# One core, attention into an ELU network: the first batch's q in paired slots with 128x128 transposes, k's maxima spread by a copy in place of diagonals, and two exchanges in the order of loads and weights

## The chip, the cores and the metric

The kernel runs on one core of a Trainium2 chip. The metric is the device time of one execution in microseconds (us). The engines that matter here: TensorE (PE in the profile, with its weight loads as PEld), VectorE (DVE), ScalarE (ACT), GpSimd (POOL) and SyncE (SP). SP and POOL also issue the loads: SP those of q, k and v, POOL those of the two weight matrices.

## The reference

q, k and v are float32 of 8 batches, 8 heads, 576 tokens and 64 columns; w_in is 512 x 2048 and w_out 2048 x 512.

```python
q_s = np.exp(q - np.max(q, axis=-1, keepdims=True))
q_s = q_s / (np.sum(q_s, axis=-1, keepdims=True) + 1e-09)
k_s = np.exp(k - np.max(k, axis=2, keepdims=True))
k_s = k_s / (np.sum(k_s, axis=2, keepdims=True) + 1e-09)
kv = np.einsum('bhsd,bhse->bhde', k_s, v)
attn = np.einsum('bhsd,bhde->bhse', q_s, kv)
x = attn.transpose(0, 2, 1, 3).reshape(8 * 576, 512)
h = x @ w_in
g = np.where(h > 0.0, h, np.exp(np.minimum(h, 0.0)) - 1.0)
out = g @ w_out
```

q's softmax runs over the 64 columns of a head, k's over the 576 tokens: k's maximum is one number for each head and column.

## The kernel before

Every batch's attention is computed while the network of the batch before it runs. The network works in steps, 16 for each batch: in a step, four hidden products (`hidden`, L912) make 128 of the 2048 hidden columns for 512 tokens, ACT, POOL and DVE apply the ELU, and four output products (`project`, L933) of an earlier step follow, three steps behind. The remaining 64 tokens of every batch are gathered and run at the end as a ninth block. PE does these products from about 20 us to the end.

The order of everything else is written out by hand. `START` lists, word by word, what is issued ahead of the first step; each engine takes its own words in that order and waits on semaphores for what it reads. `FIRST`, `SECOND` and `LATER` list, for each of the 16 steps, what is put in after the hidden products, after the output products and after the ELU. Words such as `load:Q:0:1` (load slot 1 of batch 0's q, issued by SP), `w1:14:16` (load chunks 14 and 15 of w_in, issued by POOL), `qmax`, `qsub`, `qexp`, `qsum`, `qmul` (the steps of q's softmax) and `att`, `xc` (q times kv, and its copy to XT, the input of the network) stand for methods of that name.

**The first batch.** Its q, k and v lie in four slots each. A slot holds two heads, one on partitions 0 to 63 and one on 64 to 127; a partition holds 9 tokens of its head, 8 of which belong to the 512 and one to the rest. Slot x holds heads 2x and 2x+1. Half A is slots 0 and 1, half B slots 2 and 3.

**q.** DVE takes the maxima (L672), POOL or DVE subtracts them (L679), ACT takes the exponential (L684), DVE sums (L689), and POOL or DVE multiplies by the reciprocal into QS (L708). `qturn_slots` transposes QS on PE (L766) so that the 64 columns of two partner heads lie on the partitions: four 64x64 transposes for each of the 8 tokens of a half, and eight for the rest (`pturn0:R`, in step 10). ACT copies the result to QT (L788; the rest L855).

**k.** `kmax_first` takes the maximum over a slot's 9 tokens on DVE in four steps (L326): 8 tokens to 4, to 2, to 1, and the ninth. `kturn_first` transposes the result on PE (L331), and DVE takes the maximum over the 64 partitions of a head, negated, into NM (L337): one number for each column on the partitions, a column of NM for each head of the slot pair. To subtract it, the maximum must be spread over all tokens. `kdiag` on ACT writes NM on the diagonal of a 128x128 block, one for each of the two columns (L368). `kraw_first` had put k itself into PSUM by a product with the identity (L513), and `kmin_first` adds the negated maxima there: two products for each bank (L524), with the stationary matrices HALF0 and HALF1 (ones in one half of the columns, zeros in the other) and the diagonal blocks as the moving side. A bank holds 512 columns, or 128 for the ninth tokens (parts S and T). ACT takes the exponential out of PSUM (L538, L533).

`kspread` (L465) does the same for batch 1 in step 8: two products of 256 columns, which ACT copies to NB.

**kv and what follows.** `kv_first` (L560) makes kv of a half. It needs k's exponential of that half and v's copy in bf16: `vconv:A` on ACT (L855), `vconv:B` on POOL (L857). `kv_fac` takes the reciprocal of the sums on DVE (L614) and scales kv into MB, half A on DVE (L629), half B on ACT (L623). `att` (L805) multiplies with QT, and `xc` copies to XT (ACT L814, DVE L812).

**POOL's order in the start**: subtraction of q's slot 0, the loads of w_in chunks 1 to 3 and 0, of w_out 0 and 1, of w_in 4 and 5, the subtractions of slots 2 and 3, two more weight loads, `vconv:B`, the last two multiplications of q.

Of the kernel before, what the change touches and what calls it, by code (L numbers as in the profile page):

```python
# [15 lines left out]
R = 4  # L16
# [25 lines left out]
START = ("load:Q:0:1 load:K:0:0 load:K:0:1 warm:1:7 warm:4:7 qmax:1 warm:2:4 load:Q:0:3 qsub:1:dve "  # L42
# [13 lines left out]
    4: ("w1:12:14", "w2:9:11 w2:11:13", "load:K:1:R qsum:A qsub0:R:dve"),  # L56
    5: ("w1:14:16", "kturn", "kacross vconv:R qmax:C"),
# [63 lines left out]
class Gen:  # L121
# [57 lines left out]
    def alloc(self):  # L179
# [4 lines left out]
        self.HALF = [a(f"HALF{i}", [128, 128], F32R) for i in range(2)]  # L184
# [27 lines left out]
        self.DG = a("DG", [128, 4, 128], F32R)  # L212
        self.NM = a("NM", [128, 4], F32)
        self.QM = a("QM", [128, 36], F32)
# [13 lines left out]
    def init(self):  # L228
# [17 lines left out]
        for i in range(2):  # L246
            h = self.HALF[i]
            op("dve", lambda: v.memset(h[:, 64 * i:64 * i + 64].bitcast(F32), 1.0), (), [f"HALF{i}"])
            op("dve", lambda: v.memset(h[:, 64 - 64 * i:128 - 64 * i].bitcast(F32), 0.0), (), [f"HALF{i}"])
# [17 lines left out]
    def load(self, which, b, parts, en="sp"):  # L267
# [4 lines left out]
        if b == 0 or (b == 1 and which != "Q"):  # L272
            own = "KG" if (which, b) == ("K", 1) else which + "F"
            for x in "".join({"A": "01", "B": "23", "M": "0123", "R": ""}.get(x, x) for x in parts):
                dst = t[:, QN * int(x):QN * (int(x) + 1), :].rearrange("p r d -> p (r d)")
                frm = src[b, 2 * int(x):2 * int(x) + 2, :, :].rearrange("h (p r) d -> (h p) (r d)", r=QN)
                self.op(en, lambda: e.dma_start(dst, frm), (), [f"{own}{x}"] + [f"{which}FR{x}"] * (which == "Q"), dma=f"d_{own}{x}")  # L277
            return
# [48 lines left out]

    def kturn_first(self, part, bank):
# [33 lines left out]
    def kdiag(self, en="dve", part=""):  # L362
        v, a = self.E["dve"], self.E["act"]
        f0, f1 = self.span(part)

        def fill():
            for f in range(f0, f1):
                last = a.activation(self.DG[:, f, :], self.ID32[:, :], AF.Copy,  # L368
                                    scale=self.NM[:, f:f + 1])
            return last  # L370
        if en == "act":
            self.op("act", fill, self.halves("NM", part) + ["ID32"], self.halves("DG", part))
            return
        n = f1 - f0
        self.op(en, lambda: self.E[en].tensor_tensor(
            self.DG[:, f0:f1, :], self.ID32[:, :].unsqueeze(1).broadcast_to([128, n, 128]),
            self.NM[:, f0:f1].unsqueeze(2).broadcast_to([128, n, 128]), ALU.mult),
            self.halves("NM", part) + ["ID32"], self.halves("DG", part))
# [79 lines left out]
    def kspread(self):  # L458

        pe = self.E["pe"]  # L460
        dg = self.DG[:, :, :].rearrange("p (P a) t -> p a P t", a=2)

        def mm():
            for a in range(2):
                last = pe.matmul(self.bank[AB][:, 0:256], self.HALF[a][:, :], dg[:, a], start=(a == 0), stop=(a == 1))  # L465
            return last
        self.op("pe", mm, ["HALF0", "HALF1", "DGA", "DGB"], [f"bank{AB}"])
# [48 lines left out]
    def kmin_first(self, part, banks):  # L516
        pe, P = self.E["pe"], "ABST".index(part) % 2
        n = 4 if part in "AB" else 1
        for bank in banks:
            ps = self.bank[bank][:, 0:n * 128].rearrange("p (r c) -> p r c", r=n)  # L520

            def mm():
                for a in range(2):
                    last = pe.matmul(ps, self.HALF[a][:, :],  # L524
                                     self.DG[:, 2 * P + a, :].unsqueeze(1).broadcast_to([128, n, 128]),
                                     start=False, stop=(a == 1))
                return last
            self.op("pe", mm, ["HALF0", "HALF1", f"DG{'AB'[P]}"], [f"bank{bank}"])
# [220 lines left out]
    def qturn_slots(self, part, bank):  # L749
# [3 lines left out]
        if part == "R":  # L753
            src, reads = [self.QSR[:, 2 * x:2 * x + 2, :] for x in range(2)], ["QSR"]
        else:
            hh = "AB".index(part)
            v = self.QS[hh][:, :, :, :].rearrange("p r h d -> p (r h) d").rearrange("p (r u) d -> p r u d", u=2)
            src, reads = [v[:, r, :, :] for r in range(QF)], [f"QS{2 * hh + x}" for x in range(2)]
        n = len(src)

        def mm():
            for i, x in enumerate(src):
                for k in range(4):
                    u, h = k // 2, slice(64 * (k % 2), 64 * (k % 2) + 64)
                    o = 64 * (2 * i + u if part == "R" else u * n + i)
                    last = pe.transpose(ps[h, o:o + 64], x[h, u, :], self.ID16[h, h])  # L766
            return last
# [250 lines left out]
    def do(self, j, words):  # L1018

        n = j + 1  # L1020
        plain = {"kturn": self.kturn, "kacross": self.kacross, "diag": lambda: self.kdiag("act"),
# [76 lines left out]
    def first_batch(self):  # L1098
# [7 lines left out]
        for word in START.split():  # L1106
# [5 lines left out]
            elif name == "kmax":  # L1112
                self.kmax_first(*args)
            elif name == "vconv":
# [93 lines left out]
```

## Time and profile before

| | us |
|---|---|
| runs of the kernel before (3): median | 309.31 |
| lowest and highest | 308.99, 309.39 |
| the profiled execution | 309.2 |
| its span on the core | 307.4 |
| PE busy in it | 298.6 |
| DVE, ACT, POOL busy | 234.8, 193.1, 171.8 |

The span runs from the first instruction to the end of the last one, and the profiled execution's time lies 1.8 us above it. Rows of a timeline give the start, the length, the engine, the line, the operation with its output and inputs, the shape and a count; what stands in brackets is how long the engine had been idle before it, and what ended that. Lengths of products on PE include their way through the array, so they overlap; the distance of two starts tells what one of them costs. A row of a stretch of time gives, for each engine in the order PE, PEld, DVE, ACT, POOL, the busy time and the count of instructions, and then the granted clock, the share of the transfers and their rate.

### The profile page before, as it was taken

What the parts mean: (1) busy time and instruction counts of PE and PEld (TensorE: products, weight loads), DVE (VectorE), ACT (ScalarE), POOL (GpSimd) and SP (SyncE); (2) the same over time, 40 slices, a digit from 0 to 9 for tenths busy, and PEclk for the clock granted to TensorE, in tenths of its full rate; (3) what the DMA queues carried; (4) which work ended last, traced back from release to release, by engine and by line L of the source; (5) the groups of instructions that cost most, each with busy time, mean ns of one, the idle gap of its engine ahead of it and who ended that gap; (6) DMA issues with size and microseconds to landing.
All of it is one profiled execution on the core that took longest, in us unless ns stands there. A gap on an engine that the chain in (4) does not pass through costs nothing.

```text
span 307.4 us, 4838 instructions
## 1 busy us (share of the span) xinstructions
PE 298.6 (97%) x1733; PEld 240.5 (78%) x1733; DVE 234.8 (76%) x400; ACT 193.1 (63%) x358; POOL 171.8 (56%) x215
## 2 busy tenths in 40 slices
PE   7789999999999999999999999999999999999995
PEld 5467877788878888888888888888888888888884
DVE  6888988979959897999799988998895353335442
ACT  2588885586559684967487758775877543334432
POOL 2877884687437643785378627863786333333440
PEclk9999999999999999999999999999999999999999
DMA  7999999994708993768475846590512030003004
GB/s 233 396 345 373 377 350 265 297 265 115 188 15 250 258 254 102 226 126 230 121 230 135 218 126 221 139 197 0 173 29 51 2 136 0 0 2 136 0 0 136
DMA packets 60071, 51.63 MB, mean 168 GB/s; under 512 B 26896, under 2 KB 50192, under 8 KB 60048
## 3 DMA queue, kind: packets, MB, share of 16 engines
q1 hardware_dynamic: 52960, 41.23, 48.0%
q0 software_dynamic: 5888, 8.39, 10.1%
q10 hardware_dynamic: 1200, 1.72, 2.0%
q8 instruction: 13, 0.21, 0.3%
q14 instruction: 10, 0.08, 0.1%
HBM read 38.27 MB, written 9.45 MB: 155 GB/s over the span
## 4 chain that ended last, share of the span: by engine, by line
PE 91%; POOL 3%; DVE 2%; DMA 2%; issue 1%; SPq 1%; ACT 0%
PE bank L933 43%; PE bank L912 42%; PE bank L827 2%; DMA QR<-in_q_dram 2%; PE bank L598 1%; POOL W1S L255 1%; DVE KT L326 1%; POOL QR L679 1%; PE bank L560 1%; SPq L277 1%; PE bank L805 1%; POOL W2S L262 0%; POOL VB L857 0%; DVE QM L672 0%; PE bank L1007 0%
## 5 line engine op out<-in xcount | busy, mean ns | idle before, releaser
L933 PE MATMUL bank<-W2S,GT 128*128 128x512 f32 x572 | 153.4, 391 | 0.1
L896 POOL TENSOR_SCALAR ES<-ES 128x512 f32<-128x512 f32 (+1 forms) x130 | 86.3, 666 | 115.8 <-ACT ES L895 115.8
L912 PE MATMUL bank<-XT,W1S 128*128 128x512 f32 x512 | 138.5, 393 | 0.5 <-issue 0.2
L925 DVE SCALAR_TENSOR_TENSOR GT<-bank,ES 128x512 fp32r<-128x512 f32 (+1 forms) x130 | 87.9, 680 | 53.2 <-PE bank L912 40.4
L933 PEld LDWEIGHTS bank<-W2S,GT 128*128 128x128 f32 x572 | 106.3, 188 | 22.0 <-DVE GT L925 0.6
L895 ACT ACTIVATE ES<-bank 128x512 f32<-128x512 f32 (+1 forms) x130 | 76.1, 593 | 70.5 <-PE bank L912 70.4
L912 PEld LDWEIGHTS bank<-XT,W1S 128*128 128x128 f32 x512 | 94.0, 188 | 20.0 <-ACT XT L814 0.9
L679 POOL TENSOR_TENSOR QR<-QR,QM 128x512 f32<-128x512 f32 (+1 forms) x21 | 24.9, 1190 | 1.0 <-DVE QM L672 1.0
L684 ACT ACTIVATE QR<-QR 128x1024 f32<-128x1024 f32 (+3 forms) x19 | 19.0, 1007 | 3.5 <-DVE QR L679 3.5
L855 ACT ACTIVATE XT<-bank 128x320 fp32r<-128x320 f32 (+1 forms) x30 | 15.1, 502 | 9.4 <-PE bank L827 9.2
L689 DVE TENSOR_REDUCE QZ<-QR 128x16 f32<-128x1024 f32 (+1 forms) x14 | 18.8, 1343 | 0.6 <-ACT QR L684 0.6
L672 DVE TENSOR_REDUCE QM<-QR 128x16 f32<-128x1024 f32 (+1 forms) x14 | 18.8, 1344 | 0.3 <-DMA QR<-in_q_dram 0.3
L912 PE MATMUL bank<-XTR,W1S 128*128 128x512 f32 x64 | 16.6, 389 | 0.0
L438 DVE TENSOR_TENSOR KR<-KR,NB 128x512 f32<-128x512 f32 x16 | 14.6, 936 | 0.0
L623 ACT ACTIVATE MB<-bank,KZ 64x64 fp32r<-64x64 f32 x44 | 10.1, 302 | 7.0 <-DVE KZ L614 6.9
L387 DVE TRANSPOSE_TENSOR_REDUCE KM<-KR 128x32 f32<-128x1024 f32 x12 | 14.4, 1224 | 0.0
L912 PEld LDWEIGHTS bank<-XTR,W1S 128*128 128x128 f32 x64 | 12.0, 188 | 2.5
L857 POOL CAST QT<-QW 128x1024 fp32r<-128x1024 f16 x12 | 12.5, 1045 | 2.5 <-DMA QW<-QS 2.5
L827 PE MATMUL bank<-QT,MB 128*128 128x320 f32 (+1 forms) x48 | 12.6, 302 | 0.7 <-ACT XT L855 0.7
L892 ACT ACTIVATE ES<-bank 128x512 f32<-128x512 f32 x15 | 8.9, 595 | 6.4 <-PE bank L912 6.4
L708 POOL TENSOR_TENSOR QS<-QR,QI 128x1024 f16<-128x1024 f32 (+1 forms) x7 | 12.5, 1790 | 0.3 <-DVE QI L691 0.3
L484 ACT ACTIVATE EK<-KR 128x1024 bf16<-128x1024 f32 x12 | 12.6, 1050 | 0.0
(108 smaller groups left out, 264.3 us busy)
## 6 DMA issues: line engine op xcount, KB each, us to landing
out_dram<-OSB SPq DMA_DIRECT2D x30, 256.0 KB, 2.8
KR<-in_k_dram SPq DMA_DIRECT2D x6, 1024.0 KB, 8.2
VR<-in_v_dram SPq DMA_DIRECT2D x6, 1024.0 KB, 6.3
QR<-in_q_dram SPq DMA_DIRECT2D x5, 1024.0 KB, 8.0
W2S<-in_moe_w_out_dram POOLq DMA_DIRECT2D x5, 512.0 KB, 11.4
KR<-in_k_dram SPq DMA_DIRECT2D x8, 288.0 KB, 6.4
VR<-in_v_dram SPq DMA_DIRECT2D x8, 288.0 KB, 6.5
W1S<-in_moe_w_in_dram POOLq DMA_DIRECT2D x3, 768.0 KB, 9.5
```

The source lines that it names most:

```text
L438: self.op(en, lambda: e.tensor_tensor(kv, kv, m, ALU.subtract), keys + ["NB"], keys)
L672: self.op("dve", lambda: v.tensor_reduce(m, QR, AX.X, ALU.max), self.qkeys(b, part), self.qstat("QM", b, part))
L679: self.op(en, lambda: e.tensor_tensor(QR, QR, m, ALU.subtract), keys + self.qstat("QM", b, part), self.qown(b, part))
L684: self.op("act", lambda: a.activation(QR, QR, AF.Exp), keys, self.qown(b, part))
L689: self.op("dve", lambda: v.tensor_reduce(z, QR, AX.X, ALU.add), self.qkeys(b, part), self.qstat("QZ", b, part))
L827: last = pe.matmul(self.bank[bank][:, a - c0:b - c0], self.MB[f][:, :, :].rearrange("p u d -> p (u d)"), self.QT[:, f, a - f * S:b - f * S ...
L855: self.op("act", lambda: e.activation(out, src, AF.Copy), reads, writes)
L895: self.op("act", lambda: a.activation(ES[:, x], ps[:, x], AF.Exp), [f"bank{bank}"], keys + mark)
L896: self.op("gp", lambda: g.tensor_scalar(ES[:, x], ES[:, x], -1.0, 1.0, ALU.add, ALU.mult), keys, keys)
L912: return pe.matmul(ps, self.W1S[:, kc, c * 128:(c + 1) * 128], x[:, kc, 0:SM], start=(kc == 0), stop=(kc == 3))
L925: self.op("dve", lambda: v.scalar_tensor_tensor(out[:, x], *how), [f"bank{bank}"] + eks + (["FINE"] if n < FINE else []), keys)
L933: return pe.matmul(self.bank[OB[t]][:, :], self.GT[n % NG][:, t * 128:(t + 1) * 128], self.W2S[:, c, :], start=(c == 0), stop=(c == NCH - ...
```

## The change

- **q's slots.** The four loads of the first batch's q take other heads: for a half P, slot 2P+u holds heads 4P+u (on partitions 0 to 63) and 4P+2+u (64 to 127). The partner heads of a transposed block so lie in neighbouring slots on the same partitions, and a 128x128 transpose of both turns them at once: 8 transposes for a half in place of 32, and 2 for the rest in place of 8. Their results are put in the same places of QT.
- **k's maxima.** `kdiag` becomes `kwide`: ACT copies NM, each of its columns repeated 64 times, to NMW (128 x 128 for a half). In `kmin_first` NMW is the stationary side and the identity IDR the moving one, one product for each bank. `kspread` so makes two products of 128 columns in place of two of 256. HALF0 and HALF1, which DVE filled by four memsets, are gone; POOL copies the identity to IDR.
- **The maxima of slots 2 and 3.** The first step (8 tokens to 4) stays one for each slot (`kmh`), and the other three are made for both slots at once (`kmt:B`).
- **Two exchanges in the order.** SP issues q's slot 0 ahead of slot 3. POOL issues w_in chunks 14 and 15 in step 4 and w_out chunks 11 and 12 in step 5; before it was the other way round.

```diff
-START = ("load:Q:0:1 load:K:0:0 load:K:0:1 warm:1:7 warm:4:7 qmax:1 warm:2:4 load:Q:0:3 qsub:1:dve "
-         "load:Q:0:0 kmax:0 warm:3:5 load:K:0:2 kraw:A qexp:1 kmax:1 load:K:0:3 kturn:A load:V:0:1 "
-         "qmax:0 kraw:S qsum:1 qsub:0:gp kacross:A load:Q:0:2 kmax:3 kraw:B kmax:2 kmax2:R "
+START = ("load:Q:0:1 load:K:0:0 load:K:0:1 warm:1:7 warm:4:7 qmax:1 warm:2:4 load:Q:0:0 qsub:1:dve "
+         "load:Q:0:3 kmax:0 warm:3:5 load:K:0:2 kraw:A qexp:1 kmax:1 load:K:0:3 kturn:A load:V:0:1 "
+         "qmax:0 kraw:S qsum:1 qsub:0:gp kacross:A load:Q:0:2 kmh:3 kraw:B kmh:2 kmt:B kmax2:R "
...
-    4: ("w1:12:14", "w2:9:11 w2:11:13", "load:K:1:R qsum:A qsub0:R:dve"),
-    5: ("w1:14:16", "kturn", "kacross vconv:R qmax:C"),
+    4: ("w1:12:14", "w2:9:11 w1:14:16", "load:K:1:R qsum:A qsub0:R:dve"),
+    5: ("w2:11:13", "kturn", "kacross vconv:R qmax:C"),
...
-        for i in range(2):
-            h = self.HALF[i]
-            op("dve", lambda: v.memset(h[:, 64 * i:64 * i + 64].bitcast(F32), 1.0), (), [f"HALF{i}"])
-            op("dve", lambda: v.memset(h[:, 64 - 64 * i:128 - 64 * i].bitcast(F32), 0.0), (), [f"HALF{i}"])
+        op("gp", lambda: g.tensor_copy(self.IDR[:, :], self.ID32[:, :]), ["ID32"], ["IDR"])
...
+                P, u = int(x) // 2, int(x) % 2
                 frm = src[b, 2 * int(x):2 * int(x) + 2, :, :].rearrange("h (p r) d -> (h p) (r d)", r=QN)
+                if which == "Q":
+                    frm = src[b, 4 * P:4 * P + 4, :, :].rearrange("(a u) (p r) d -> u a p (r d)", u=2, r=QN)[u]
...
+    def kmax_half(self, part):
+
+        v, x = self.E["dve"], int(part)
+        src = self.KR[0][:, x * QN:(x + 1) * QN, :]
+        T = self.KT2[:, 4 * (x % 2):4 * (x % 2) + 4, :]
+        self.op("dve", lambda: v.tensor_tensor(T, src[:, 0:4, :], src[:, 4:8, :], ALU.max),
+                self.firstkeys("K", part), [f"KT2{'AB'[x % 2]}"])
+
+    def kmax_tail(self, part):
+
+        v, P = self.E["dve"], "AB".index(part)
+        src = self.KR[0][:, 2 * P * QN:2 * (P + 1) * QN, :].rearrange("p (u r) d -> p u r d", r=QN)
+        T = self.KT2[:, :, :].rearrange("p (u r) d -> p u r d", r=4)
+        kt, ka = ["KT2A", "KT2B"], [f"KA{2 * P}", f"KA{2 * P + 1}"]
+        out = self.KA[:, 2 * P:2 * P + 2, :]
+        steps = ((T[:, :, 0:2, :], T[:, :, 0:2, :], T[:, :, 2:4, :], kt, kt), (
+            T[:, :, 0, :], T[:, :, 0, :], T[:, :, 1, :], kt, kt), (
+            out, T[:, :, 0, :], src[:, :, 8, :], self.firstkeys("K", part) + kt, ka))
+        for o, p, q, reads, writes in steps:
+            self.op("dve", lambda: v.tensor_tensor(o, p, q, ALU.max), reads, writes)
...
-    def kdiag(self, en="dve", part=""):
-        v, a = self.E["dve"], self.E["act"]
+    def kwide(self, en="act", part=""):
+
         f0, f1 = self.span(part)
...
+        src = self.NM[:, f0:f1].unsqueeze(2).broadcast_to([128, f1 - f0, 64])
+        self.copy(en, self.NMW[:, f0:f1, :], src, self.halves("NM", part), self.halves("NW", part))
+
+    def across(self, P):
+
+        return self.NMW[:, 2 * P:2 * P + 2, :].rearrange("p a g -> p (a g)")
...
-            for a in range(2):
-                last = pe.matmul(self.bank[AB][:, 0:256], self.HALF[a][:, :], dg[:, a], start=(a == 0), stop=(a == 1))
+            for P in range(2):
+                last = pe.matmul(self.bank[AB][:, 128 * P:128 * P + 128], self.across(P), self.IDR[:, :],
+                                 start=True, stop=True)
...
-            def mm():
-                for a in range(2):
-                    last = pe.matmul(ps, self.HALF[a][:, :],
-                                     self.DG[:, 2 * P + a, :].unsqueeze(1).broadcast_to([128, n, 128]),
-                                     start=False, stop=(a == 1))
-                return last
-            self.op("pe", mm, ["HALF0", "HALF1", f"DG{'AB'[P]}"], [f"bank{bank}"])
+            self.op("pe", lambda: pe.matmul(
+                ps, self.across(P), self.IDR[:, :].unsqueeze(1).broadcast_to([128, n, 128]),
+                start=False, stop=True), ["IDR", f"NW{'AB'[P]}"], [f"bank{bank}"])
...
-            for i, x in enumerate(src):
-                for k in range(4):
-                    u, h = k // 2, slice(64 * (k % 2), 64 * (k % 2) + 64)
-                    o = 64 * (2 * i + u if part == "R" else u * n + i)
-                    last = pe.transpose(ps[h, o:o + 64], x[h, u, :], self.ID16[h, h])
+            for x, o in zip(src, out):
+                last = pe.transpose(o, x.rearrange("p u d -> p (u d)"), self.ID16[:, :])
```

38 lines of the change are left out of this document (15 added, 23 removed).

## The prediction

> **What bounds the kernel.** I read the page's first part, then the chain of waits of the first 27 us, then the engines' timelines there, and last TensorE's timeline between 35 and 42 us.
>
> ```profile
> PE 298.6 (97%) x1733; PEld 240.5 (78%) x1733; DVE 234.8 (76%) x400; ACT 193.1 (63%) x358; POOL 171.8 (56%) x215
> ```
>
> PE is busy for 298.6 of 307.4 us. Once its stream of hidden and output products runs, only work taken out of that stream, or an earlier start of it, can shorten the span. So two questions remain: what sets the start, and what the change takes out of the stream.
>
> ```profile
> 2.60 5.53 DMA QR<-in_q_dram
> 8.16 0.70 DVE QF L672
> 8.93 1.04 POOL QR L679
> ...
> 16.44 1.16 POOL VB L857
> 17.73 0.76 PE bank L560 x36
> ```
>
> This is the chain of waits (start, length, what). q's slot 0 is issued at 2.60 and lands at 8.13; DVE takes its maximum; POOL subtracts it from 8.93 on. From there the chain stays on POOL (subtractions and the issues of weights, back to back) up to the end of v's conversion (vconv:B) at 16.44 + 1.16 = 17.60, and only then can PE make the second half of kv (17.73). What follows kv (its scaling on ACT, the first att copy, the first hidden product) hangs on that moment.
>
> ```profile
> 13.70 0.69 ACT L368 ACTIVATE DG<-ID,NM 128x128 fp32r<-128x128 f32 x2 [0.44 <-DVE NM L337]
> ...
> 17.25 0.29 ACT L533 ACTIVATE EK<-bank 128x128 bf16<-128x128 f32 x1
> 18.82 1.04 ACT L623 ACTIVATE MB<-bank,KZ 64x64 fp32r<-64x64 f32 x4 [0.36 <-DVE KZ L614]
> ```
>
> ACT is a close second: after its wait for NM it runs without a gap to 17.54 (kexp:T, the other thing kv:B needs), 0.06 before POOL. Both must come earlier, or nothing is won. After kv:B, ACT waits for KZ (18.82) ahead of the first XT copy, so this stretch moves with kv:B.
>
> **The start: the loads swapped.** SP now issues slot 0 ahead of slot 3.
>
> ```profile
> 2.13 0.91 SPq L277 DMA_DIRECT2D QR<-in_q_dram  x2
> ```
>
> ```profile
> DMA to landing us min/median/max: 5.3/5.3/5.3
> ```
>
> ```profile
> 8.16 0.69 DVE L672 TENSOR_REDUCE QF<-QR 128x8 f32<-128x512 f32 x1 [0.64 <-DMA QR<-in_q_dram]
> ...
> 9.75 0.50 DVE L326 TENSOR_TENSOR KT<-KR 128x256 f32<-128x256 f32 x1
> ...
> 12.19 1.27 DVE L672 TENSOR_REDUCE QF<-QR 128x8 f32<-128x512 f32 x2
> ...
> 13.11 2.08 POOL L679 TENSOR_TENSOR QR<-QR,QF 128x512 f32<-128x512 f32 x2
> 13.38 0.28 DVE L337 TENSOR_REDUCE NM<-bank 128x2 f32<-128x128 f32 x1
> ```
>
> The first row holds the issues of slots 3 and 0, the second is the time to landing of the first of them: 2.13 + 5.3 = 7.43, so slot 0 in its place lands 0.70 earlier than at 8.13. DVE had been idle for 0.64 before its maximum at 8.16, so the maximum starts near 7.5, and POOL near 8.23 in place of 8.93: **0.70 earlier**. Slot 3 takes the landing at 8.13; it is used in the pair at 12.19. POOL's chain moves as a whole if its next input is early enough: the two subtractions at 13.11 would start at 12.4 and need slot 2's maximum, the first of the two at 12.19. That depends on the DVE work ahead of it.
>
> **k's maxima on DVE.** Two chains of four steps become two first steps and a joint tail of three. By the groups of instructions, kept apart by shape, over the first 25 us:
>
> ```profile
> L326 DVE TENSOR_TENSOR KT<-KR 128x256 f32<-128x256 f32 x4 | 1.8, 440 | 0.0
> L326 DVE TENSOR_TENSOR KT<-KT 128x128 f32<-128x128 f32 x6 | 1.8, 292 | 0.2
> L326 DVE TENSOR_TENSOR KT<-KT 128x64 f32<-128x64 f32 x4 | 0.9, 225 | 0.1
> L326 DVE TENSOR_TENSOR KT<-KT 128x256 f32<-128x256 f32 x2 | 0.8, 424 | 0.1
> ```
>
> The last step, into KA, is as long as one of KT of its width. Before: 2 x (440 + 292 + 225 + 225) = 2364 ns. After: 2 x 440 + 424 + 292 + 292 = 1888 ns. The saving is 0.48. It can't start much before 9.75, since PE waits for the same landing of k until 9.76 (below). From 9.70, with the measured 12.19 - 9.75 = 2.44 less 0.48, slot 2's maximum runs from 11.66 to 12.35, against POOL's 12.4: level with it, so I keep 0.70 for POOL. The negated maxima NM of half B (13.38) come 0.53 earlier; kturn:B, which they need, isn't late, as PE ahead of it loses a product.
>
> **The copy for the diagonals.** ACT wrote two 128x128 diagonals in 0.69 per half; one broadcast copy of the same 128 columns replaces them. The trace has no such copy. Bounds: the 128x128 exponential at 17.25 took 0.29, the pair 0.69. I take half the pair, 0.35. With NM at 13.13, ACT starts about 13.2 and is through at 13.55 in place of 13.70 + 0.69 = 14.39; from there it has no wait, so kexp:T ends near 16.7, ahead of POOL's 17.60 - 0.70 = 16.90. The exponentials need the spreading product on PE, now one per bank in place of two, so PE isn't later. ACT then isn't last, and **kv:B moves by 0.70**. The other copies of this kind (half A; the four diagonals of batch 1) save ACT time that nothing waits for.
>
> Edits at nothing: the four memsets on DVE ran while it waited for q's first slot; IDR's copy on POOL falls in POOL's 6.5 us of idleness before 8.93. If that cover were gone, each would cost some 0.3. The 128x128 transposes in the start (8 for 32) are covered too: after pturn:A PE waits for POOL, and after pturn:B for XT on ACT. The q loads read the same bytes in two pieces of two heads; no row shows that form. Bounds: no difference, or the gain by the swap is lost (a rival).
>
> **In PE's stream.**
>
> ```profile
> 9.76 0.67 PE L513 MATMUL bank<-KR,ID 128*128 128x512 f32 x1 [0.52 <-DMA KR<-in_k_dram]
> 15.48 0.33 PE L524 MATMUL bank<-DG,HALF 128*128 128x128 f32 x2
> 15.74 0.76 PE L560 MATMUL bank<-VB,EK 64*64 64x66 bf16 x36
> ...
> 35.57 0.40 PE L465 MATMUL bank<-DG,HALF 128*128 128x256 f32 x2
> 35.81 1.09 PE L912 MATMUL bank<-XT,W1S 128*128 128x512 f32 x4
> 36.74 0.62 PE L744 MATMUL bank<-ID,QS 128*128 128x128 f16 x8
> 37.17 1.17 PE L933 MATMUL bank<-W2S,GT 128*128 128x512 f32 x4
> 38.17 1.07 PE L912 MATMUL bank<-XT,W1S 128*128 128x512 f32 x4
> 39.08 1.07 PE L933 MATMUL bank<-W2S,GT 128*128 128x512 f32 x4
> 40.08 0.31 PE L766 MATMUL bank<-ID,QSR 64*64 64x64 f16 x8
> 41.35 0.53 PE L864 MATMUL bank<-QT,MB 128*128 128x64 f32 x4
> ```
>
> The first row is PE's wait for k. kspread (35.57): two products of 256 columns took 0.24, 0.12 each; now two of 128 columns. The two of 128 columns at 15.48 took 0.26 up to the next row, 0.13 each. So a product of half the columns isn't shorter in this type, and I count **0**; the bounds are half of 0.24 saved, and 0.02 lost. The Trainium skill, TensorE: Matmul & The Clock Gate, section Back-to-back issue gap, gives 134 cycles for 128 columns and 262 for 256; by that estimate 0.12 would be saved. The trace doesn't agree (0.13 against 0.12 us), and the measurement decides.
>
> The rest's transposes (40.08): a group of four products alone takes 39.08 - 38.17 = 0.91. From 39.08 to 41.35 are 2.27 for two groups and eight 64x64 transposes: these cost 0.45. From 35.81 to 38.17 are 2.36 for two groups and eight 128x128 ones: 0.54, at 0.054 a piece (0.43 from 36.74 to 37.17). Two of these cost 0.54 - 6 x 0.054 = 0.22. **Saved 0.23**; bounds 0 and 0.45.
>
> The weights, moved on POOL's queue: w1's last two chunks are issued before two of w2.
>
> ```profile
> L255 POOL DMA_DIRECT2D W1S<-in_moe_w_in_dram x1: 796/796/796, 30.7 to 30.7; - x1
> ...
> DMA to landing us min/median/max: 17.4/17.4/17.4
> ```
>
> ```profile
> 48.17 1.20 PE L912 MATMUL bank<-XT,W1S 128*128 128x512 f32 x4
> ```
>
> w1's load issued at 30.7 lands at 48.1, and PE uses it at 48.17: no slack. An earlier stream would wait right there and give everything back; with the two exchanged it lands in the earlier place, and w2's chunk 11, needed by the products at 49.99, takes the landing at 48.1, with 1.9 of slack before and 0.9 after the move. So this edit costs nothing (the issues are 0.80 and 0.73 long on POOL) and keeps the gain.
>
> **Sum.** 0.70 + 0.23 = 0.93 us, against the profiled execution's own 309.2 us (span 307.4 and 1.8 around it): 308.3. The median of the runs is 309.31, 0.1 above; from it I get 308.4. **Predicted 308.3.**
>
> **Rivals.** (1) ACT sets kv:B. If NM isn't earlier, or the copy is as long as the pair, ACT gains between 0 and 0.35 where POOL gains 0.70. For it: 0.06 between the two today. Against it: NM's 0.53. Price: 0.35 + 0.23 = 0.58, giving **308.7**. (2) The two-piece load isn't earlier, or is served more slowly, so slot 0 lands at 8.13 as before. POOL stays; only the rest's transposes pay: **309.1**. Nothing in the trace speaks for it but that it shows no such load. (3) On the other side, PE falls to half rate.
>
> ```profile
> 1.68 4.64 PE L1093 MATMUL bank<-GT,ONES 128*128 128x512 f32 x10 [1.68 <-DVE VBR L240]
> 14.00:16.00 2.00, 1.56 (x22) 1.31 (x24) 1.93 (x3) 2.00 (x6) 2.00 (x4) 1.00 1.15 371
> 16.00:18.00 2.00, 1.30 (x81) 1.21 (x76) 1.90 (x7) 2.00 (x5) 2.00 (x3) 1.00 1.21 359
> ```
>
> The first ten products took 0.46 each, twice the 0.23 of the stream: PE begins at half rate and stays there for at least 4.6 us. Between 14 and 18 PE is busy for 2.86 of 4 us; the change takes out two products of 0.23 and one of 0.13 there, which leaves about 2.3. If this is too little, PE runs at half rate for another 4.6 us from 18 on. With the same share of work there, 2.86 of 4, that loses 4.6 x 0.72 / 2 = 1.6 us; less the gain of 0.93, **309.9**. It decides from the point at which the share of work between the spreading products and kv:B is too small to hold the rate. Against it: PE still works every microsecond or two. The same page of the Trainium skill, Part 1, says that an idle window of about 3.4 us halves the clock, and Part 4 that transposes don't count as work; no run here shows that limit.
>
> **Chances.** Forecast 0.58 (own range 308.0 to 308.6), rival 1 0.20, rival 2 0.07, rival 3 0.15. A measurement of this kernel tells 0.2%, 0.62 us, from no change: faster means under 308.69. The forecast gives 0.56 of its share to faster, rival 1 half of its 0.20; together 0.66. Same: 0.02 + 0.10 + 0.07 = 0.19. Slower: 0.15. The range 307.8 to 309.4 takes in both bounds of the transposes and of kspread (0.34 below the forecast at most) and rivals 1 and 2, and leaves out rival 3.
>
> **What would show it.** slot 0's maximum at 7.45 and POOL at 8.2; the copy on ACT at 0.3 to 0.4 and kexp:T's end before POOL's conversion; kv:B at 17.0; the first L933 at 24.5 in place of 25.20; from the group before the rest's transposes to the one after, 0.23 less; no wait at the fifteenth hidden product. Wrong if kv:B follows ACT, if products after 14 us are spaced by 0.4, or if a weight's landing ends an idle time of PE after 25 us.

## The result and the profile after

| | before | after |
|---|---|---|
| median of the runs | 309.15 | 335.52 |
| lowest and highest | 308.78, 309.39 | 334.87, 336.24 |
| span of the profiled execution | 307.4 | 333.4 |
| PE busy in it | 298.6 | 302.1 |
| start of the first output product | 25.20 | 51.59 |

Times in us. The ratio is 1.0855, with an interval of 1.0828 to 1.0882: the change costs 26.4 us, and it costs them all ahead of the first output product, which comes 26.39 later. From there to the end of the span it takes 281.8 us after and 282.2 before. This isn't yet a gain of the change: in the runs below that stretch lies between 281.9 and 282.2 with and without the wider transposes (but for one, at 283.9).

First the windows of the start (in each row the window, its length, busy time of PE, PEld, DVE, ACT and POOL, the granted clock, the share of the 16 DMA engines that is busy, GB/s). The kernel before, one row:

```profile
5.00:10.00 5.00, 4.48 (x12) 2.23 (x11) 4.12 (x14) 0.77 (x2) 1.07 (x2) 1.00 1.02 366
```

The kernel after:

```profile
5.00:10.00 5.00, 1.32 (x4) 0.50 (x2) 0.37 (x1) 0.00 (x0) 0.00 (x0) 1.00 0.13 51
10.00:15.00 5.00, 3.81 (x7) 1.71 (x7) 3.17 (x10) 0.63 (x1) 0.00 (x0) 1.00 0.31 99
15.00:20.00 5.00, 0.06 (x1) 0.00 (x0) 1.64 (x4) 0.42 (x2) 1.36 (x2) 0.78 0.49 150
20.00:30.00 10.00, 4.29 (x9) 2.25 (x9) 1.77 (x5) 0.68 (x2) 2.80 (x4) 0.50 1.12 280
```

The loads are slow and the DMA engines are idle at the same time: a share of 0.13 is 2 engines of 16, and they move 51 GB/s. A load of a q slot is 128 pieces of 2304 bytes, 294,912 bytes; at 51 GB/s that is 5.8 us in place of the 0.70 between the landings of slots 3 and 0 before. Next, SP's own timeline of the kernel after:

```profile
0.74 0.73 SPq L277 DMA_DIRECT2D QR<-in_q_dram  x1
1.52 0.89 SPq L277 DMA_DIRECT2D KR<-in_k_dram  x2
2.46 5.13 SPq L277 DMA_DIRECT2D QR<-in_q_dram  x2
7.63 6.24 SPq L277 DMA_DIRECT2D KR<-in_k_dram  x2
...
15.20 10.75 SPq L277 DMA_DIRECT2D VR<-in_v_dram  x3
```

The issues of two loads of k and of three of v, whose form did not change, take 6.24 and 10.75 us: they stand behind q's loads. Who waits for them is seen on DVE and PE of the kernel after:

```profile
9.63 0.69 DVE L681 TENSOR_REDUCE QF<-QR 128x8 f32<-128x512 f32 x1 [7.47 <-DMA QR<-in_q_dram]
...
17.87 0.69 DVE L681 TENSOR_REDUCE QF<-QR 128x8 f32<-128x512 f32 x1 [4.46 <-DMA QR<-in_q_dram]
...
37.75 1.28 DVE L681 TENSOR_REDUCE QF<-QR 128x8 f32<-128x512 f32 x2 [10.28 <-DMA QR<-in_q_dram]
```

```profile
25.71 3.75 PE L526 MATMUL bank<-KR,ID 128*128 128x512 f32 x4 [10.65 <-DMA KR<-in_k_dram]
...
40.33 1.33 PE L535 MATMUL bank<-IDR,NMW 128*128 128x512 f32 x3 [9.16 <-ACT NMW L863]
41.59 1.20 PE L569 MATMUL bank<-VB,EK 64*64 64x66 bf16 x36
```

Slot 0's maximum is at 17.87 instead of the forecast 7.45, k's slot 3 reaches PE at 25.71 instead of 9.76. The wait for NMW at 40.33 is a wait for v: ACT writes that copy behind its conversion of v, and the chain of waits of the kernel after has v's landing ahead of both.

```profile
15.20 23.69 DMA VR<-in_v_dram
38.92 1.17 ACT VB L863
40.09 0.20 ACT NMW L863
```

An earlier v alone would have won less than 1 us there: q's slot 2, the last of the four q loads, reaches DVE at 37.75, and NM of half B, which the copy needs, comes behind the maxima of slots 2 and 3, at 38.95. With so little work PE also falls to half rate (clock 0.50 between 20 and 30, and again between 40 and 45), so kv's 36 products take 1.20 in place of 0.76.

### The profile page after: what moved, and what is told of

Its sections match the earlier page's. It is cut to its first block, busy times and chain, and to the rows that moved or that the text cites. A ratio compares the mean times of both kernels' runs of the same rounds, so it can differ in the third digit from the quotient of the medians.

```text
span 333.4 us, 4708 instructions
## 1 busy us (share of the span) xinstructions
PE 302.1 (91%) x1673; PEld 242.0 (73%) x1673; DVE 234.3 (70%) x393; ACT 191.8 (58%) x353; POOL 171.7 (51%) x216
## 3 DMA queue, kind: packets, MB, share of 16 engines
q1 hardware_dynamic: 52904, 41.23, 44.5%
## 4 chain that ended last, share of the span: by engine, by line
PE 85%; DMA 7%; SPq 4%; DVE 2%; ACT 1%; issue 1%
PE bank L941 39%; PE bank L920 39%; DMA VR<-in_v_dram 7%; SPq L277 4%; PE bank L835 2%; PE bank L607 1%; PE bank L569 1%; DVE KT L326 1%; PE bank L813 0%; PE bank L535 0%; ACT VB L863 0%; PE bank L774 0%; PE bank L1015 0%; PE bank L753 0%; DVE QM L681 0%
## 5 line engine op out<-in xcount | busy, mean ns | idle before, releaser
L526 PE MATMUL bank<-KR,ID 128*128 128x512 f32 (+1 forms) x12 | 8.3, 835 | 15.5 <-DMA KR<-in_k_dram 15.5
L688 POOL TENSOR_TENSOR QR<-QR,QF 128x512 f32<-128x512 f32 x3 | 3.1, 1038 | 31.7 <-DVE QF L681 31.7
L681 DVE TENSOR_REDUCE QF<-QR 128x8 f32<-128x512 f32 (+1 forms) x5 | 3.1, 630 | 22.2 <-DMA QR<-in_q_dram 22.2
L526 PEld LDWEIGHTS bank<-KR,ID 128*128 128x128 f32 x12 | 3.2, 304 | 19.4 <-issue 13.3
```

Of the source, the lines that this page charges most:

```text
L681: self.op("dve", lambda: v.tensor_reduce(m, QR, AX.X, ALU.max), self.qkeys(b, part), self.qstat("QM", b, part))
L688: self.op(en, lambda: e.tensor_tensor(QR, QR, m, ALU.subtract), keys + self.qstat("QM", b, part), self.qown(b, part))
```

## The experiments

Theory 1 was that the source of q's loads is what costs: its outermost count is 2 (the two heads), where before a load was 128 rows, and that count decides how many DMA engines serve a load. The rivals: that pieces far apart are slow in themselves, or that the loss needs the changed order of work too. Beside it, what the rest of the change is worth had to be found without the loads. Medians are set against runs of the kernel before on the same chip (309.0 to 309.2 in all of them); not all the runs below are of one chip, so small differences between them are read with the ratios beside them.

**Each q slot by two loads.** The changed kernel, each load cut into one for each half of the partitions:

```diff
-                self.op(en, lambda: e.dma_start(dst, frm), ...)
+                def both():
+                    for i in range(2):
+                        ins = e.dma_start(dst[64 * i:64 * i + 64], src[b, 4 * P + 2 * i + u, :, :]...)
```

> The changed kernel, with each of the first batch's four q slots loaded by two transfers of 64 partitions (one for each of its two heads) in place of one transfer of two pieces. Theory 1 (the two-piece load runs on 2 of the 16 DMA engines: in the changed kernel the DMA share from 5 to 10 us is 0.13, about 2/16, and the four loads leave 56 packets fewer, 4 x 14): the share is near 0.9 from 2.5 us on, the packets of the hardware queue rise to 53,024 (52,960 and 4 x 16), and the kernel shows what the rest of the change is worth: 308.3, as the prediction's sum had it, or up to 309.0 if SP's four more issues of 0.43 us delay k. Rival A (the slow part is the new order or the new placing of heads in slots, not the form of the transfer): it stays above 330. The Trainium skill, DMA: Bandwidth & Descriptors, section Why a DMA increments its semaphore by 16 and not by 1, says that the number of engines is the largest one up to 16 that divides the outermost sizes of both sides; that gives 2 for the changed load and 16 for this one.

Measured: 312.14 (310.87 to 313.13), ratio 1.0105 [1.0086, 1.0124]. The 23 us are gone, but the time is 3.1 over the upper end of what was expected. SP's timeline of this kernel, then its window from 6 to 8 us:

```profile
3.10 2.39 SPq L282 DMA_DIRECT2D QR<-in_q_dram  x4
5.54 1.06 SPq L289 DMA_DIRECT2D KR<-in_k_dram  x2
```

```profile
6.00:8.00 2.00, 1.71 (x3) 0.78 (x3) 1.84 (x7) 0.63 (x1) 0.00 (x0) 1.00 1.01 256
```

The issues ahead, three more than before and 0.6 us each, put that of k's slots 2 and 3 at 5.54 in place of 3.08, and while halves are on their way the engines move less: 256 GB/s at a share of 1.01 from 6 to 8 us, where the kernel before moved 369 GB/s at 0.99. The first output product comes at 27.41, 2.21 later than before. The stretch behind it is the one of 283.9 us, 1.7 longer than before; the largest single part of that is a wait of PE for a load of w_in:

```profile
29.32 1.20 PE L932 MATMUL bank<-XT,W1S 128*128 128x512 f32 x4 [0.72 <-DMA W1S<-in_moe_w_in_dram]
```

The Trainium skill, DMA: Bandwidth & Descriptors, section Rules for kernel authors, advises against two transfers to the two halves of the partitions, since both use the same engines; this run agrees, with all engines busy (1.01) and less moved.

**Only the outermost count.** The kernel before, nothing changed but the source of q's loads of batch 0. With 2 blocks the source is that of the change; with 4 blocks it takes 32 rows of each of four heads. Each run has one of the two lines. q's values then stand in other tokens' or heads' places, so the output is another one.

```diff
+                if which == "Q":
+                    frm = src[b, 4 * P:4 * P + 4, :, :].rearrange("(a u) (p r) d -> u a p (r d)", u=2, r=QN)[u]      # 2 blocks
+                    frm = src[b, 4 * P:4 * P + 4, 0:288, :].rearrange("h (p r) d -> h p (r d)", r=QN)                 # 4 blocks
```

> The kernel before with nothing changed but q's four loads of batch 0, which take the change's source (two heads that are two heads apart, outermost count 2). q's values then stand in other heads' places, which leaves the output other than the reference's. Theory 1 (two engines serve each of these loads and hold up everything behind them): 331 to 336, the whole of the loss, DMA share about 0.13 in 5 to 10 us. Rival (the loss needs the changed order of the work as well): under 325.

> The kernel before with the first batch's q slots each loaded in four blocks of 32 partitions (the first half of the tokens of four heads), so that other heads and tokens of q land in the slots than the reference has there. Theory 1: four DMA engines carry each load, 73.7 KB each at the 25 GB/s that an engine moves (about 400 GB/s over 16), 2.9 us in place of 0.72; slot 0 lands behind three such loads of q and two of k at about 14.7 in place of 8.13, so 6.6 to 8 us more: 316 to 318. Rival C (what is slow is that the source isn't one contiguous stretch): four blocks are as slow as two or slower, 330 and above.

Measured: 332.77 with 2 blocks, 321.93 with 4 (one run each), so 23.7 and 12.9 above the kernel before. The windows from 5 to 10 us, 2 blocks and then 4:

```profile
5.00:10.00 5.00, 0.96 (x4) 0.43 (x2) 0.43 (x1) 0.00 (x0) 0.00 (x0) 0.88 0.13 51
```

```profile
5.00:10.00 5.00, 1.43 (x5) 0.64 (x3) 1.57 (x3) 0.16 (x1) 0.00 (x0) 0.96 0.78 221
```

The form of the loads alone makes nearly the whole loss, and twice the blocks halve it. The share of 0.78 with 4 blocks isn't that of q's loads alone: k's loads, 128 rows each, run in the same window. The 4-block time is 4 to 6 above the expectation; PE's clock, 0.70 from 10 to 15 us and 0.64 from 15 to 20, may be part of that.

**The same pieces, nested the other way.** This is the run that decides between count and distance: the changed kernel with the 64 rows outermost and the two heads inside. Partition 2p + a then holds row p of head a, and the copies to QT read every other column.

```diff
-                    frm = ....rearrange("(a u) (p r) d -> u a p (r d)", u=2, r=QN)[u]
+                    frm = ....rearrange("(a u) (p r) d -> u p a (r d)", u=2, r=QN)[u]
...
-            src = ps[:, :].rearrange("p (j t) -> p j t", j=2)
+            src = ps[:, :].rearrange("p (t j) -> p j t", j=2)
```

> The change whole, but with q's two pieces nested the other way round: the source runs over 64 rows first and over the two heads inside, so partition 2p + a holds row p of head a, and the two copies to QT take every other column. Same bytes, same 128 pieces of 2304 bytes, same number of loads as in the changed kernel. Theory 1 (the outermost count of the source sets how many DMA engines serve a load; 2 before this edit, 64 with it): slot 0's load lands near 7.1, DMA share above 0.9 in 5 to 10 us, and the time falls by more than 24 us, to 308.3 if PE keeps its rate and to 309.3 to 309.9 if PE falls to half rate between 17 and 21 us as in the run with q undone; I take 309.6. Rival C (pieces of one load that lie 294912 bytes apart are served slowly): above 330, as the changed kernel.

Measured: 310.05 (309.69 to 312.04), ratio 1.0043 [1.0028, 1.0059]. Its window from 5 to 10 us:

```profile
5.00:10.00 5.00, 3.50 (x11) 1.53 (x11) 4.62 (x15) 1.19 (x3) 1.50 (x2) 1.00 1.00 355
```

The same bytes in the same 128 pieces, equally far apart, and 25.5 us are back. The queue's packets count the engines: 52,960 here and in the kernel before, 52,904 in the changed one and with 2 blocks, 52,912 with 4. Over four loads that is 14 fewer per load, and 12 fewer: 16 less the number of engines. The Trainium skill, DMA: Bandwidth & Descriptors, section Why a DMA increments its semaphore by 16 and not by 1, states the rule: a load runs on the largest number of engines up to 16 that divides the slowest dimension of both sides. The runs agree for 2 (0.13 of the engines) and for 64 (all); for 4 only the packets show it. Rival C, that the distance of the pieces makes them slow, fails here.

**q undone.** The changed kernel with slots, loads and transposes of q as before; left are the swapped loads, the joint maxima, the copies and the exchange of weights.

```diff
-                if which == "Q":
-                    frm = src[b, 4 * P:4 * P + 4, :, :]...
...
-                last = pe.transpose(o, x.rearrange("p u d -> p (u d)"), self.ID16[:, :])
+                for k in range(4): ...
+                    last = pe.transpose(ps[h, o:o + 64], x[h, u, :], self.ID16[h, h])
```

> The changed kernel with the q part undone: q's slots hold heads 2x and 2x+1 and are loaded as before, and q is turned by 64x64 transposes. What stays: the copy in place of the diagonals, the joint tail of k's maxima, slot 0 ahead of slot 3, and w1's last chunks ahead of w2's. Theory 1: all of the loss is gone; the start's gain of the prediction stands (kv:B 0.7 us earlier), the gain on the rest's transposes doesn't: 308.6. Rival A (order, copy or k's maxima cost something): above 310.

Measured: 309.76 (309.24 to 310.74), ratio 1.0031 [1.0019, 1.0043]: a loss of 0.7 against the kernel before on its chip (309.06), where a gain was expected. The 25 us of the loads are back; neither number of the expectation came. Its timelines of PE and DVE, and the window from 17 to 21 us:

```profile
14.07 0.76 PE L567 MATMUL bank<-VB,EK 64*64 64x66 bf16 x36 [0.19 <-ACT EK L545]
16.34 0.69 PE L773 MATMUL bank<-ID,QS 64*64 64x64 f16 x32 [1.51 <-DVE QS L715]
17.43 1.05 PE L567 MATMUL bank<-VB,EK 64*64 64x66 bf16 x36 [0.40 <-POOL VB L864]
```

```profile
7.47 0.68 DVE L679 TENSOR_REDUCE QF<-QR 128x8 f32<-128x512 f32 x1
...
12.33 0.28 DVE L356 TENSOR_REDUCE NM<-bank 128x2 f32<-128x128 f32 x1
...
13.48 2.81 DVE L715 TENSOR_TENSOR QS<-QR,QF 128x1024 f16<-128x1024 f32 x1
...
18.62 0.17 DVE L621 RECIPROCAL KZ<-bank 128x2 f32<-128x2 f32 x1
```

```profile
17.00:21.00 4.00, 3.60 (x75) 2.74 (x72) 2.96 (x9) 2.64 (x6) 3.56 (x5) 0.58 1.31 321
```

Two things are seen. PE's clock is 0.58 of full from 17 to 21: kv:B takes 1.05. And DVE's product into QS, 1.76 in the kernel before, takes 2.81: it begins 1.05 earlier and ends where it did, at 16.29. So the reciprocal KZ of half B, behind it on DVE, stands at 18.62, where it stood before too (ACT's copies, which wait for it, begin at 18.82 in both).

**Holding PE's rate.** Four products more, whose result nobody reads, where PE waited 1.5 us, in the kernel with q undone and in the one with nested rows:

```diff
-... kv:A kfac:A:dve pturn:A kv:B "
+... kv:A kfac:A:dve warm:4:3 pturn:A kv:B "
```

> The change with q undone (309.76 before) and the same four products. Theory 1: granted clock 1.00 from 17 to 21, the first output product at 24.6 in place of 25.87, and 308.4 to 308.8. Rival D: 309.5 to 310.0.

> The same with four more products of 512 columns on PE, whose result nobody reads, after kv:A and ahead of pturn:A, where PE waits 1.5 us for DVE. Theory 1 (the start loses by PE's half rate, because too little is left for PE between 14.8 and 17.4 us): granted clock 1.00 from 17 to 21, kv:B's 36 products in 0.76, first output product at 24.4 to 24.7, and 308.1 to 308.6. Rival D (the rate isn't the cause, or four products don't hold it): no earlier than the kernel without them, 309.3 to 309.9.

Measured: 308.97 (308.56 to 309.5), ratio 1.0000 [0.9990, 1.0010], and 309.61 (309.15 to 309.86), ratio 1.0017 [1.0007, 1.0027]. The first one's window:

```profile
17.00:21.00 4.00, 3.43 (x75) 2.36 (x75) 3.35 (x11) 3.18 (x7) 3.12 (x4) 1.00 1.31 322
```

The rate holds, also in all 24 executions of the two (mean clock 0.998 or more, 0.989 to 0.994 in all nine with q undone alone), and 0.79 and 0.44 come back: half rate was real, at a half and a quarter of the price that rival 3 had. The times are above theory 1's all the same, the second one in the range of rival D, with the first output products at 24.73 and 25.64. The rest of the forecast gain is still missing.

**The swap alone.** The kernel before with slot 0 ahead of slot 3:

```diff
-... qmax:1 warm:2:4 load:Q:0:3 qsub:1:dve load:Q:0:0 kmax:0 ...
+... qmax:1 warm:2:4 load:Q:0:0 qsub:1:dve load:Q:0:3 kmax:0 ...
```

> The kernel before with q's slot 0 loaded ahead of slot 3, and nothing else. The prediction's reading of the start: POOL begins 0.7 us earlier, but ACT, whose wait for NM hangs on k's third and fourth landing, still ends k's exponentials at about 17.5 us, so kv:B moves by less than 0.1: 309.1. Rival B (POOL alone sets kv:B): 0.7 is won, 308.5.

Measured: 308.77 (308.28 to 309.18), ratio 0.9991 [0.9982, 1.0000]. DVE, then PE:

```profile
7.44 0.68 DVE L672 TENSOR_REDUCE QF<-QR 128x8 f32<-128x512 f32 x1
```

```profile
17.29 0.76 PE L560 MATMUL bank<-VB,EK 64*64 64x66 bf16 x36 [0.58 <-ACT EK L533]
...
24.70 1.19 PE L933 MATMUL bank<-W2S,GT 128*128 128x512 f32 x4
```

The swap works: slot 0's maximum is 0.72 earlier, kv:B 0.44, and now ACT's exponential is last ahead of kv:B. The first output product is 0.50 earlier. The time lies between the expectation and rival B: ACT was last as expected, but it ended its exponentials 0.30 earlier too, and 0.13 of that is only k's slot 3, which reached PE at 9.63 in this profile and at 9.76 in that of the kernel before.

**Why the product into QS is slow.** Theory 2: it now begins beside POOL's subtractions of slots 2 and 3. First these subtractions were moved to DVE, in both kernels that hold PE's rate:

```diff
-... qsub:2:gp qsub:3:gp diag:act:B ...
+... qsub:2:dve qsub:3:dve diag:act:B ...
```

> The kernel with q undone and the four products (308.97), and the subtractions of q's slots 2 and 3 moved from POOL to DVE, so that POOL does no arithmetic while DVE multiplies slots 0 and 1 into QS. Theory 2 (that product took 2.81 us in place of 1.57 to 1.76 because it now begins beside POOL's subtractions, and this keeps the reciprocal of kv's sums on DVE, for which ACT waits after kv:B, where it was): the product takes 1.1 to 1.4 us although it begins 1.2 later, the reciprocal KZ of half B stands some 0.4 to 0.6 earlier than at 18.16, the first output product at 24.1 to 24.4 in place of 24.73, and the time is 308.2 to 308.6. Rival E (the product is long for another reason; DVE just gets 1.2 us more work): the product stays above 2.5, KZ comes 1.2 later, and the time is 309.5 to 310.2.

> The same move in the changed kernel with q's two pieces nested the other way and the four products (309.61). Theory 2: the product at 1.1 to 1.4 us, the first output product at 25.0 to 25.3 in place of 25.64, 309.0 to 309.3. Rival E: 310.2 to 310.9. What is left above the kernel with q undone is by theory 1 SP's longer issues (0.57 to 0.67 us each in place of 0.43), which land k's slots later, less the 0.25 of the rest's transposes.

Measured: 308.98 (308.56 to 310.4), ratio 1.0003 [0.9991, 1.0015], and 309.85 (309.02 to 312.21), ratio 1.0047 [1.0024, 1.0070]. The first one's DVE:

```profile
14.42 1.28 DVE L715 TENSOR_TENSOR QS<-QR,QF 128x1024 f16<-128x1024 f32 x1
...
18.03 0.17 DVE L621 RECIPROCAL KZ<-bank 128x2 f32<-128x2 f32 x1
```

and its POOL, which ends v's conversion 0.18 after the product's start:

```profile
13.42 1.18 POOL L864 CAST VB<-VR 128x1152 bf16<-128x1152 f32 x1
```

Theory 2 was right on the product, 1.28 in place of 2.81 (1.48 in the second kernel). It was wrong on the time: the two subtractions cost DVE 1.28 themselves, so its queue ends hardly earlier and nothing is won. The second median isn't of the move alone: five of its twelve executions took 311.2 to 312.2 us at a mean clock of 0.987 to 0.994, the other seven 309.0 to 310.2 at 1.00. Then DVE's queue was reordered, with KZ ahead of q's sums of slot 3:

```diff
-... qmul:A:dve qsum:2 ... qsum:3 ... kv:A kfac:A:dve ... kv:B pwide:A:act kfac:B:act ... qmul:3:gp pturn:B ...
+... qmul:A:dve ... kv:A kfac:A:dve qsum:2 ... kv:B pwide:A:act kfac:B:act qsum:3 ... qmul:3:dve pturn:B ...
```

> The kernel with q undone, the four products and the subtractions on DVE (308.98), with DVE's order changed after the product into QS: the scaling of kv's half A and the reciprocal KZ of half B stand ahead of q's sums of slots 2 and 3 as far as their inputs allow, and DVE multiplies slot 3 in POOL's place. Theory 3 (DVE's queue, with q's sums ahead of KZ, sets the first XT copies once kv:B is early): KZ of half B at 17.3 to 17.5 in place of 18.03, ACT's MB copies near 17.6 in place of 18.23, the first hidden product at 19.6 to 19.8 in place of 20.00, 308.5 to 308.8. Rival F (the multiplication of slot 3 and its transposes on PE, which now come later, set the first hidden product): 308.9 to 309.4, with PE waiting for DVE's QS ahead of the second group of transposes.

Measured: 308.96 (308.65 to 310.52), ratio 0.9995 [0.9981, 1.0010]: rival F. PE of this kernel:

```profile
19.71 0.69 PE L773 MATMUL bank<-ID,QS 64*64 64x64 f16 x32 [0.81 <-DVE QS L715]
```

What was taken from ahead of KZ is waited for at q's second group of transposes. KZ itself stood at 17.94, where 17.3 to 17.5 had been expected.

Last, the early start itself was undone: the kernel with q undone and the four products (308.97), with k's maxima in two chains as before, so that DVE comes to the product later.

```diff
-... kmh:3 kraw:B kmh:2 kmt:B kmax2:R ...
+... kmax:3 kraw:B kmax:2 kmax2:R ...
```

> The kernel with q undone and the four products (308.97), and k's maxima of slots 2 and 3 in two chains of four steps as before: left of the change are the swapped loads, the copy in place of the diagonals and the exchange of weights. Theory 2 (the 0.48 us saved on k's maxima is worth nothing, because it only lets DVE's product into QS begin beside POOL's subtractions): the product takes 1.5 to 1.8 us in place of 2.81, KZ of half B stands, counted from the landing of k's slot 3, where it does with the joint maxima or up to 0.3 earlier, and the time is 308.6 to 309.0. Rival G (the joint maxima do carry a gain): 309.2 to 309.6, KZ 0.4 later than 9.29 us behind that landing.

Measured: 308.54 (308.3 to 308.89), ratio 0.9990 [0.9981, 0.9999], the lowest median of all kernels here, though by the ratios level with the swap alone (0.9991). DVE and POOL of the kernel with joint maxima:

```profile
12.15 2.08 POOL L686 TENSOR_TENSOR QR<-QR,QF 128x512 f32<-128x512 f32 x2
13.02 2.81 DVE L715 TENSOR_TENSOR QS<-QR,QF 128x1024 f16<-128x1024 f32 x1
...
18.16 0.17 DVE L621 RECIPROCAL KZ<-bank 128x2 f32<-128x2 f32 x1
```

and with two chains:

```profile
12.50 2.04 POOL L686 TENSOR_TENSOR QR<-QR,QF 128x512 f32<-128x512 f32 x2 [0.33 <-DVE QF L679]
14.06 1.57 DVE L715 TENSOR_TENSOR QS<-QR,QF 128x1024 f16<-128x1024 f32 x1
...
17.96 0.17 DVE L621 RECIPROCAL KZ<-bank 128x2 f32<-128x2 f32 x1
```

The product begins 1.04 later (0.47 of it because k's slot 3 reached PE at 9.48 in this profile, at 9.01 in the other; the other 0.57 is DVE's longer work, 0.48 by the prediction's sum) and ends 0.20 earlier. Counted from k's slot 3, KZ is 0.67 earlier, more than theory 2 had, and the median is 0.43 lower. The two ran on different chips, and against the kernel before on each the intervals, 0.9990 to 1.0010 and 0.9981 to 0.9999, overlap: that saving this work gained nothing is shown, that it was a loss is likely.

## Why the prediction was wrong, by its own steps

- **The q loads (the step that failed).** "The q loads read the same bytes in two pieces of two heads; no row shows that form. Bounds: no difference, or the gain by the swap is lost (a rival)." The upper bound was 0.70 us; the form costs 25.5 (335.52 against 310.05 with the rows outermost). Rival 2 named the step, "is served more slowly", but priced it as if one landing came later by one load's length. No row of the trace of before shows such a load; the 2 engines of 16 that were measured make 0.70 x 16 / 2 = 5.6 us of each q load, and of the wait of all that stands behind it in SP's order. By the rule of the Trainium skill, DMA: Bandwidth & Descriptors, that is quoted above, the 2 engines could have been foreseen, and the 5.6 us with them, as an estimate.
- **The swap.** 0.70 forecast, 0.72 measured at slot 0's maximum. "kv:B moves by 0.70" was not: it came 0.44 earlier in the run with the swap alone, where ACT became last, as rival 1 had it, and 0.30 earlier with q undone (17.43), where POOL's conversion of v, 1.56 long in place of 1.16, was last. With the four products it came 0.75 earlier (16.98, in a profile in which k's slot 3 was 0.75 earlier too), and with the subtractions on DVE 1.46 earlier (16.27); the ratios there are 1.0000 and 1.0003. So an early kv:B alone isn't a gain.
- **k's maxima.** The saving on DVE is there, NM of half B comes earlier, and the time is no better (308.97 with it, 308.54 without). What failed is "after kv:B, ACT waits for KZ ..., so this stretch moves with kv:B": KZ is DVE's, and its queue holds the product into QS and q's sums ahead of KZ. The prediction followed POOL, ACT and PE to kv:B and not DVE, and left out DVE's product into QS (1.76 before), whose length depends on what POOL does meanwhile.
- **The copy for the diagonals.** 0.35 forecast, 0.30 measured in the run with q undone.
- **Rival 3, half rate.** It came in both kernels in which q's loads were early and no products were added (q undone, nested rows). It lasted 3.4 us in both profiles (17.7 to 21.1 and 18.5 to 21.9), where 4.6 were taken, and the price, 1.6 in the forecast, was 0.79 and 0.44.
- **The stream.** With q undone and with nested rows the first output product starts at 25.87 in both profiles, so the two can be compared directly; the output products behind the rest's transposes, first with q undone, then with nested rows:

```profile
25.87 1.20 PE L940 MATMUL bank<-W2S,GT 128*128 128x512 f32 x4
...
42.41 1.17 PE L940 MATMUL bank<-W2S,GT 128*128 128x512 f32 x4
```

```profile
25.87 1.20 PE L940 MATMUL bank<-W2S,GT 128*128 128x512 f32 x4
...
36.25 0.33 PE L477 MATMUL bank<-IDR,NMW 128*128 128x128 f32 x2
36.42 1.13 PE L919 MATMUL bank<-XT,W1S 128*128 128x512 f32 x4
...
42.14 1.17 PE L940 MATMUL bank<-W2S,GT 128*128 128x512 f32 x4
```

Up to here the rest's transposes save 0.27 (0.23 forecast). kspread costs 0.17 in place of 0.24 in the kernel before; 0.07 is saved where 0 was taken, inside the bounds. But "only work taken out of that stream, or an earlier start of it, can shorten the span" isn't enough: the stream waits as well. At 80 us, first with q undone, then with nested rows:

```profile
80.00 0.31 PE L834 MATMUL bank<-QT,MB 128*128 128x320 f32 x1
```

```profile
80.05 0.38 PE L834 MATMUL bank<-QT,MB 128*128 128x320 f32 x1 [0.16 <-POOL QT L864]
```

The 0.27 is gone there: PE waits for a later batch's QT, which POOL copies out of a transfer; that copy began at 78.86, with q undone at 77.35. From the first output product to PE's wait for XT some 61 us behind it, the kernels with 128x128 transposes took 61.21 (the changed kernel), 61.34, 61.51 and 61.52 (but for the one with two loads for each slot), those with 64x64 transposes 61.36 to 61.57. The ranges overlap: the term of 0.23 was right where it was measured, and by then little or nothing was left of it.

Without the failed loads the change would still have been slower than forecast, 310.05 against 308.3. The differences of medians give about 0.44 of it to half rate and, across two chips, 0.43 to the joint maxima. Paired slots in their good form cost another 0.64 (309.61 against 308.97, on one chip); SP's issues of the nested source, 0.57 to 0.67 us in place of 0.43, put the issue of k's slots 2 and 3 at 3.81 in place of 3.08 and may be the reason, which wasn't tried by itself. The changed kernel is 2.8 above the kernel before with the same loads. Of that, 2.57 stand at the first output product (51.59 against 49.02), and v lands at 38.89 in place of 34.77:

```profile
15.14 19.63 DMA VR<-in_v_dram
```

This is v's row in the chain of the kernel before with 2 blocks; the changed kernel's is shown above. In the changed kernel slot 0 comes earlier (its maximum is at 17.87, there at 22.98), so POOL issues the weights from 19.62 on instead of 24.74, while v is still on its way. That they hold v up is likely, but no run tried it.

## What to carry to other kernels

Before a load's source or destination is rearranged, look at the outermost count of both sides: here a copy of the same bytes ran on 2 DMA engines instead of 16, and all that followed in the same queue waited with it; the same pieces, nested so that the large count stood outside, brought it back. Follow every engine's queue to the point where the stretches meet, not only the engine that is last today; work saved on one engine may let its next instruction collide with another engine's. Where a change thins out PE's work in a start, price the lower clock and fill the gap. And look for the stream's next wait behind a saving: what is saved ahead of it can be waited away there.

## What the runs showed of the hardware

- **DVE and POOL hold each other up.** The same product of 128x1024 on DVE took 1.28 with POOL's subtractions out of the way, 1.57 and 1.76 where POOL's subtractions ended 0.5 and 0.7 us after its start, and 2.81 in the four profiles where they went on for 0.9 to 1.2 us; POOL's conversion of v took 1.56 beside it in place of 1.16. The shorter lengths follow one sum: 1.10 plus the time that POOL's instruction ran on (0.13, 0.18, 0.39, 0.49 and 0.66 us gave 1.23, 1.28, 1.48, 1.57 and 1.76), as if DVE stood still meanwhile. The Trainium skill, GPSIMD Engine Reference, section Key points, says that GpSimd shares its ports to the on-chip memory with VectorE instructions that have two inputs there; the runs agree. By the sum 2.81 would be 2.0 to 2.3; why it is longer stays open.
- **PE's rate fell after a gap of 2.6 us.** With q undone, PE had transposes alone between 14.83 and 17.43, and the clock fell to 0.50 at 17.7; with nested rows the gap was 15.01 to 17.61 and the clock fell at 18.5. With the four products the longest such gap was 1.5 us, and in all profiles of kernels with them it held (in seven executions of three of these kernels it seems not to have: mean clock 0.987 to 0.994). The Trainium skill, TensorE: Matmul & The Clock Gate, Part 1, speaks of an idle window of about 3.4 us; the measured 2.6 is less.
- **Landings scatter from one execution to the next.** PE's wait for k's slot 3 ended between 9.01 and 9.79 in the profiles of the kernels with the same first seven loads as the swapped ones (q in its old form): a single profile can't tell gains below that size, and the medians here moved by less than the profiles did.
